# The jobs of an attention and mixer kernel in another written-out order, with other engines for its evacuations

## The chip, the cores and the metric

One core of a Trainium2 chip runs the whole kernel. The metric is device time in microseconds (us) from the start of an execution to its end. The engines are TensorE (PE in the profile, with weight loads as PEld), VectorE (DVE), ScalarE (ACT), GpSimd (POOL) and SyncE (SP). TensorE writes its products into PSUM, in eight banks, from which DVE or ACT (not POOL here) take them away; such a read is called an evacuation below. DMA transfers are issued from the queues of SP, ACT and POOL and carried by 16 DMA engines.

## The reference

Eight batches, eight heads, 576 positions, 64 channels a head. Attention with 128 positive random features is followed by a token and a channel mixer on rows of 512 channels.

```python
def phi(x):                        # x = q or k, scaled by 64 ** -0.25
    h = einsum('bhsd,md->bhsm', x, omega) - sum(x * x, -1) / 2
    return exp(h - max(h, -1)) / sqrt(128)
q_p, k_p = phi(q_s), phi(k_s)
kv, z = einsum('bhsm,bhsd->bhmd', k_p, v), k_p.sum(2)
x = einsum('bhsm,bhmd->bhsd', q_p, kv) / (einsum('bhsm,bhm->bhs', q_p, z) + 1e-6)
x = x.transpose(0, 2, 1, 3).reshape(8, 576, 512)
u = x + (relu(x.transpose(0, 2, 1) @ w_tok1) @ w_tok2).transpose(0, 2, 1)
out = u + relu(u @ w_ch1) @ w_ch2  # 512 -> 1536 -> 512
```

## The kernel before

Every batch is cut into 512 main positions and 64 tail positions. The kernel first describes its work as 1528 *jobs* and then issues them. A job is a function that issues a few instructions on one engine, with the jobs that it depends on, the buffers that it takes and those that it frees. `Planner.add` (L155) appends one; its number is its place in the list.

The order of issue is not found when the program is built. `Planner.run` (L182) walks a list of numbers written into the file, `ORDER` (L22), and calls each job's function in turn. Every engine and every DMA queue runs what it was issued in that order, so the list fixes the order of each engine by itself and of SP's, ACT's and POOL's queues of transfers. Two more tables go with it. `SLOT` is a string of digits: the next digit gives the buffer of its ring (or the PSUM bank) whenever a job takes a new one. `MOVED` gives the engine of jobs that do not run on their usual one; `Planner.engine` (L208) looks it up as a job is described. A negative entry n of `ORDER` is no job: it calls `warm(-1-n)` (L1251), one 128x512 product of a tensor of zeros into bank -1-n, whose result nothing reads.

```python
for n in ORDER:
    if n < 0:
        self.warm(-1 - n)
        continue
    j = self.jobs[n]
    ...
    self.go(j)
```

`turns` (L163) makes elementwise jobs of DVE and POOL that use their shared port take turns, by an explicit dependency wherever the two engines alternate.

The stages of a batch b, with the lines that the profile names:

- *Loads.* For batches 0 and 1 q and k come in as rows (L367, L378) and TensorE transposes them (L518, L535, L552). From batch 2 on POOL's queue casts them to 16 bits in DRAM (L407 for q, L412 and L418 for main and tail of k) and SP's queue brings them back transposed (L428) as qT and kT. v is loaded by POOL (L385, L399).
- *Attention.* Features of k (L599, L707) and of q (L719) are products evacuated by exponentials on ACT (L562, and others). DVE reduces (L740) and inverts (L744) for the scale of v, which is multiplied on DVE or POOL (L343, a helper for all elementwise sums and products). TensorE makes kv (L763, L770) and numerators with denominators (L796, L798); DVE inverts the denominators (L803) and DVE or ACT scale (L814, L812), which gives x.
- *Token mixing.* Products L831 and the tail L824 with relu, then L844 (L898 for a pair's tail) and on DVE the addition of x (L847), which gives u. From batch 2 on SP's queue transposes u (L852) as uT, its only wait being the four additions. Batches 0 and 1 have their own version (L870, L871, L882, L884) in which TensorE gives uT itself.
- *Channel mixing.* Batches 0 and 1: products L1178 and L1212. From batch 2 on the two products are split into 2 by 2 blocks and made as seven products of sums of blocks: L1107 on the way in with sums of uT (POOL or DVE) and of the weights, evacuated by DVE (L1131) and ACT (L338), and L989 on the way out with sums S and T of the hidden blocks (POOL or DVE, L343), added up by DVE in `o` (L969). Stores go out from SP, ACT or POOL (L1024, L1036).

The list overlaps batches: while channel mixing of one batch runs, attention of the next batch or the one after it is laid between its products. In the list before, channel mixing of batch c starts at these job numbers: 178 (batch 0), 463 (batch 2), 641 (batch 3). The jobs that the prediction speaks of by their place are 634 (transpose of u of batch 3, on SP), 717 and 893 (transposes of k of batches 4 and 5, on SP), 890 and 891 (the casts that 893 depends on, on POOL), 154 (first token product of batch 0), 459 and 460 (two sums of uT of batch 2), 0 (the identity on POOL, `make_identity`) and 10 (a load of rows on POOL's queue).

Of the kernel before, what the change touches and what calls it, by code (L numbers as in the profile page):

```python
# [22 lines left out]
    2, 38, 16, 3, 7, 6, 4, 9, 12, 10, 0, -8, 41, 1, 14, 39, 42, 40, 47, 48, 8, 11, 13, 21, 22, 19, 17, 5, 78, 49,  # L23
    129, 43, 79, 80, 50, 131, 130, 44, 18, 45, 46, 95, 54, 96, 97, -1, 51, 69, -3, 112, 52, 55, 113, 114, 84, 135,
    56, 53, 28, 73, 70, 101, 118, 102, 136, 119, 120, 103, 137, 132, -8, 81, -3, 74, 71, 75, 133, 76, -1, -1, -3,
    -1, 57, 115, 82, 72, 116, 134, 59, -8, -8, -2, 104, 117, 121, 138, 98, 83, 105, 30, 25, 23, 24, 77, 20, 33, 31,
    29, 85, 58, 122, 139, 100, 99, 86, -1, 126, 140, 123, 143, 87, 88, 141, 124, 127, 125, 128, 144, 145, 63, 106,
    92, 89, 154, 109, 142, 158, 65, 159, 90, 107, 155, 93, 110, 91, 108, 94, 156, 111, 64, 208, 15, 160, 146, 161,
    147, 157, 253, 66, 209, 150, 67, 151, 255, 211, 210, 254, 68, 148, 152, 149, 153, 60, 270, 219, 178, 186, 271,
    272, 220, 221, 187, 179, 184, 212, 62, 61, 213, 259, 276, 236, 256, 216, 238, 237, 218, 258, 182, 172, 176, 180,  # L30
    217, 173, 257, 177, 214, 225, 260, 185, 277, 183, 242, 226, 243, 278, 261, 222, 239, 273, 32, 241, 240, 275,
    170, 168, 171, 27, 353, 26, 351, 215, 162, 279, 163, 262, 244, 274, 224, 280, 165, 356, 357, 263, 223, 164, 181,
    227, 284, 281, 264, 282, 265, 267, 166, 245, 174, 169, 246, 175, 167, 285, 266, 283, 247, 228, 268, 269, 229,
    286, 188, 230, 250, 233, 251, 248, 231, 252, 249, 232, 234, 235, 189, 193, 198, 287, 194, 290, 288, 289, 457,
    34, 291, 203, 294, 292, 296, 298, 199, 195, 200, 293, 295, 297, 299, 35, 36, 196, 451, 352, 355, 403, 386, 358,
    354, 453, 300, 535, 536, 190, 204, 191, 405, 201, 388, 387, 404, 420, 369, 359, 421, 361, 422, 360, 205, 370,
    389, 366, 391, 301, 303, 368, 367, 371, 304, 390, 323, 319, 320, 307, 308, 206, 315, 392, 409, 426, 362, 427,
    302, 324, 410, 393, 428, 411, 363, 364, 394, 537, 372, 406, 423, 313, 316, 424, 408, 373, 407, 425, 375, 365,
    311, 305, 429, 395, 412, 312, 376, 37, 377, 309, 306, 314, 374, 310, 396, 413, 430, 417, 418, 434, 414, 400,
    397, 431, 378, 435, 436, 401, 419, 415, 432, 321, 379, 383, 380, 416, 384, 398, 381, 385, 399, 382, 325, 317,  # L40
    402, 433, 322, 455, 452, 192, 207, 202, 538, 539, 197, 437, 550, 556, 438, 440, 542, 713, 540, 541, 714, 558,
    326, 439, 441, 551, 557, 552, 327, 454, 318, 456, 329, 331, 458, 333, 335, 336, 715, 328, 332, 334, 330, 444,
    446, 553, 570, 448, 339, 555, 554, 571, 572, 442, 445, 447, 449, 559, 443, 337, 543, 604, 587, 544, 606, 545,
    588, 605, 589, 340, 560, 576, 342, 341, 546, 338, 547, 548, 577, 343, 610, 344, 611, 450, 607, 590, 573, 592,
    609, 574, 575, 716, 717, 347, 578, 549, 561, 579, 345, 612, 459, 460, 562, 348, 593, 580, 608, 591, 563, 581,
    584, 613, 564, 567, 346, 582, 585, 565, 566, 594, 568, 569, 583, 614, 586, 463, 615, 496, 495, 618, 479, 480,
    466, 498, 468, 500, 619, 616, 620, 595, 461, 462, 617, 482, 499, 483, 501, 497, 596, 464, 469, 597, 502, 503,
    467, 484, 485, 601, 470, 598, 465, 471, 504, 602, 599, 472, 600, 486, 510, 487, 481, 488, 505, 475, 473, 506,
    603, 476, 478, 491, 489, 721, 621, 507, 492, 509, 622, 508, 723, 623, 722, 624, 474, 494, 490, 477, 493, 511,
    515, 512, 513, 625, 349, 519, 350, 891, 1068, 1244, 720, 718, 719, 895, 894, 890, 889, 517, 516, 724, 520, 630,  # L50
    631, 632, 628, 765, 768, 626, 633, 629, 627, 725, 726, 523, 767, 770, 766, 769, 524, 782, 748, 728, 784, 749,
    750, 783, 729, 730, 634, 525, 526, 734, 731, 751, 732, 752, 733, 753, 771, 772, 754, 527, 755, 531, 788, 528,
    737, 532, 738, 727, 514, 773, 756, 518, 637, 739, 893, 892, 896, 638, 1069, 774, 757, 635, 775, 735, 758, 736,
    641, 776, 762, 759, 779, 777, 763, 780, 636, 760, 789, 529, 521, 764, 761, 522, 530, 644, 778, 781, 897, 907,
    899, 908, 909, 898, 657, 642, 658, 924, 785, 790, 640, 1067, 639, 645, 660, 926, 740, 646, 787, 741, 786, 925,
    673, 674, 900, 913, 901, 661, 930, 662, 791, 643, 745, 647, 742, 648, 676, 792, 793, 663, 678, 664, 649, 679,
    677, 794, 902, 746, 795, 743, 650, 796, 653, 747, 797, 665, 680, 659, 666, 651, 903, 675, 744, 534, 1071, 533,
    681, 669, 667, 685, 798, 654, 670, 686, 652, 682, 672, 931, 668, 683, 932, 799, 941, 958, 800, 802, 942, 656,
    959, 960, 943, 801, 803, 684, 688, 655, 687, 671, 693, 689, 695, 691, 697, 698, 944, 904, 927, 946, 905, 906,
    929, 945, 808, 806, 701, 810, 804, 933, 699, 934, 928, 964, 807, 809, 811, 805, 961, 1075, 1119, 1077, 1076,  # L60
    962, 1120, 963, 1121, 812, 1070, 1074, 1072, 1249, 1073, 1245, 696, 694, 690, 702, 965, 966, 704, 935, 938, 700,
    914, 915, 947, 936, 939, 937, 948, 705, 703, 916, 940, 917, 967, 968, 692, 949, 910, 1136, 1085, 709, 911, 912,
    1086, 1137, 1087, 918, 972, 950, 951, 833, 1125, 1078, 1079, 706, 1080, 1126, 919, 710, 969, 952, 955, 973, 974,
    970, 956, 957, 953, 954, 707, 921, 817, 818, 920, 971, 1138, 922, 923, 975, 1102, 978, 820, 1104, 1103, 836,
    979, 815, 1127, 813, 814, 1142, 1143, 1144, 1248, 1081, 816, 976, 977, 822, 838, 1082, 1122, 708, 821, 1108,
    1091, 823, 1084, 1124, 1083, 986, 982, 824, 980, 1145, 1128, 983, 981, 1109, 987, 1129, 825, 839, 1123, 819,
    849, 852, 984, 834, 829, 826, 1130, 827, 840, 830, 985, 837, 854, 841, 1131, 1092, 828, 1132, 835, 842, 850,
    1133, 1134, 853, 1110, 1093, 855, 856, 831, 857, 832, 845, 851, 843, 1135, 848, 858, 844, 864, 861, 1094, 846,
    862, 1095, 1146, 859, 860, 847, 863, 1247, 712, 711, 988, 1261, 1139, 1088, 989, 1111, 990, 1112, 1263, 1262,
    1090, 1140, 1089, 1141, 873, 1278, 1251, 1105, 1252, 1279, 1253, 1107, 1106, 996, 1012, 1011, 995, 1027, 869,  # L70
    1250, 874, 871, 865, 867, 993, 991, 1113, 998, 1280, 1030, 1014, 999, 1254, 1114, 1115, 1243, 992, 994, 870,
    866, 1246, 1423, 877, 1028, 1000, 1016, 1116, 1032, 1147, 1015, 1001, 1002, 1117, 1031, 1148, 1118, 878, 1149,
    997, 1017, 1033, 1013, 1018, 1034, 1096, 1003, 1099, 1007, 1019, 1004, 1035, 1008, 880, 1005, 1284, 1100, 1020,
    1255, 1006, 1101, 1150, 1039, 1151, 1021, 879, 1029, 1097, 1256, 881, 1098, 1022, 1152, 1040, 1153, 1295, 1023,
    868, 872, 1036, 882, 1267, 1042, 1268, 1285, 885, 1154, 1037, 1156, 1026, 1009, 1296, 1024, 1025, 1297, 1157,
    1155, 883, 1038, 1301, 1041, 886, 1257, 1269, 1286, 884, 1302, 1010, 1298, 1281, 1312, 1300, 1282, 1283, 1313,
    1314, 1299, 1162, 1163, 1043, 1044, 1303, 1160, 1164, 1158, 1051, 1165, 1161, 1159, 1264, 1315, 1258, 1424, 888,
    1166, 1422, 1259, 1260, 875, 1318, 1287, 1319, 1052, 1045, 1047, 1049, 1053, 1266, 1288, 1316, 1265, 1317, 1292,
    1289, 1270, 1055, 1304, 1048, 1290, 1271, 876, 1305, 1320, 887, 1272, 1275, 1321, 1050, 1167, 1168, 1046, 1169,
    1170, 1309, 1293, 1056, 1273, 1054, 1058, 1276, 1310, 1274, 1311, 1322, 1291, 1323, 1326, 1306, 1324, 1294,  # L80
    1277, 1307, 1327, 1328, 1308, 1325, 1203, 1172, 1171, 1204, 1329, 1187, 1206, 1330, 1331, 1190, 1059, 1174,
# [1204 lines left out]
```

## Time and profile before

| | us |
|---|---|
| three runs | 268.26, 268.55, 269.92 |
| their median | 268.55 |
| the profiled execution, its own time | 270.67 |
| its span, first to last instruction | 268.9 |
| mean granted TensorE clock in it | 0.998 |
| DMA traffic | 39.72 MB in 81826 packets, mean 148 GB/s |

The page gives busy time of each engine as a share of the span. The other views used are: the waits of an engine (what ended each idle stretch: total us, times, longest), busy time in stretches (length, then each engine's busy us with its instructions, the granted clock, the mean busy share of the DMA engines, GB/s), the chain that ended last (start, length, what), and an engine's timeline (start, length, line, operation, out<-in, count, and in brackets the idle time ahead with what ended it). A DMA's line on its queue's timeline is the time the queue took to issue it; the transfer itself goes on behind that. Matmuls overlap, so busy times of neighbours in a timeline do; from start to start is the better measure.

### The profile page before, as it was taken

The numbers are of one execution on the slowest core, as the hardware profiler recorded it, in microseconds if no ns is written. First come the engines' busy times: TensorE is split into PE (matmuls) and PEld (weight loads), VectorE is DVE, ScalarE is ACT, GpSimd is POOL, SyncE is SP. The second block draws the span as 40 slices with busy tenths as digits, with TensorE's granted clock in tenths as the row PEclk, the third lists the DMA queues.
The fourth block names the chain that finished last, engine by engine and source line by source line (L and its number), as shares of the span: only waits on it lengthen the run. The fifth ranks groups of instructions, "written<-read, shape, count | busy, mean of one in ns | idle before, by whom it ended". The sixth has DMA issues, their size and how long they took to land.

```text
span 268.9 us, 6989 instructions
## 1 busy us (share of the span) xinstructions
PE 257.9 (96%) x2752; PEld 190.6 (71%) x2752; DVE 231.7 (86%) x494; ACT 183.0 (68%) x425; POOL 158.9 (59%) x160
## 2 busy tenths in 40 slices
PE   4999999999999999989999999999999999999993
PEld 2568455454667985768768777897696788888882
DVE  3999978599999998889999999998987898788982
ACT  1997982089885896879988989878865482273400
POOL 8765553061897966987498852745775004927171
PEclk9999999999999999999999999999999999999999
DMA  7999999999999999999999927844350513040144
GB/s 192 199 208 200 205 207 184 175 220 186 240 168 143 175 207 187 121 198 210 175 222 189 240 85 80 119 85 95 105 152 0 80 67 112 0 157 4 41 146 127
DMA packets 81826, 39.72 MB, mean 148 GB/s; under 512 B 64033, under 2 KB 77729, under 8 KB 81601
## 3 DMA queue, kind: packets, MB, share of 16 engines
q0 software_dynamic: 31712, 17.61, 44.7%
q1 hardware_dynamic: 48560, 19.50, 34.7%
q10 hardware_dynamic: 1520, 2.16, 2.3%
q8 instruction: 21, 0.34, 0.5%
q14 instruction: 13, 0.10, 0.1%
HBM read 35.95 MB, written 16.52 MB: 195 GB/s over the span
## 4 chain that ended last, share of the span: by engine, by line
PE 81%; DMA 7%; POOL 6%; issue 2%; DVE 2%; ACT 1%; POOLq 0%
PE bank L989 23%; PE bank L1107 21%; PE bank L1178 7%; PE bank L1212 4%; PE bank L831 4%; PE bank L844 4%; DMA k<-in_k_dram 4%; DMA uT<-u 3%; PE bank L707 3%; PE bank L796 3%; PE bank L763 2%; PE bank L719 2%; POOL S L343 2%; POOL vs L343 1%; POOL uT L343 1%
## 5 line engine op out<-in xcount | busy, mean ns | idle before, releaser
L562 ACT ACTIVATE kp<-bank 128x512 f16<-128x512 f32 x64 | 35.8, 610 | 13.5 <-PE bank L707 13.1
L338 ACT ACTIVATE r<-bank 128x512 f16<-128x512 f32 (+1 forms) x50 | 29.1, 606 | 20.1 <-PE bank L1107 9.9
L989 PEld LDWEIGHTS <-r 128*128 128x128 f16 x384 | 36.9, 98 | 6.8 <-issue 1.0
L562 ACT ACTIVATE qp<-bank 128x512 f16<-128x512 f32 x64 | 36.7, 631 | 2.5 <-PE bank L719 2.4
L740 DVE TENSOR_REDUCE km<-kp 128x8 f16<-128x1024 f16 x32 | 38.1, 1205 | 0.5 <-ACT kp L562 0.5
L343 POOL TENSOR_TENSOR vs<-v,vs 128x512 f16<-128x512 f16 x22 | 23.7, 1082 | 16.0 <-DVE vs L744 5.5
L1107 PE MATMUL bank<-uT,wc 128*128 128x256 f16 x228 | 30.5, 273 | 1.2 <-DMA uT<-u 1.2
L989 PEld LDWEIGHTS <-S 128*128 128x128 f16 x288 | 27.6, 98 | 4.4 <-POOL S L343 0.2
L1107 PEld LDWEIGHTS <-wc 128*128 128x128 f16 x252 | 23.5, 98 | 5.7 <-DMA uT<-u 1.7
L343 POOL TENSOR_TENSOR S<-r,S 128x768 f16<-128x768 f16 x15 | 24.4, 1641 | 4.5 <-DVE vbd L644 3.4
L989 PE MATMUL bank<-T,r 128*128 128x256 f16 x192 | 23.8, 273 | 0.1
L989 PE MATMUL bank<-T,S 128*128 128x256 f16 x192 | 23.6, 273 | 0.0
L989 PE MATMUL bank<-wc,r 128*128 128x256 f16 x192 | 23.4, 273 | 0.0
L812 ACT ACTIVATE x<-bank,rc 128x64 f16<-128x64 f32 x100 | 22.4, 348 | 0.4 <-DVE rc L803 0.4
L343 POOL TENSOR_TENSOR uT<-uT,uT 128x512 f16<-128x512 f16 x10 | 11.6, 1158 | 17.9 <-PE bank L1107 15.8
L338 ACT ACTIVATE r<-r 128x512 f16<-128x512 f16 (+1 forms) x21 | 16.7, 822 | 7.5 <-DVE r L1131 7.5
L1107 PE MATMUL bank<-uT,qT 128*128 128x256 f16 x126 | 21.7, 272 | 0.0
L847 DVE TENSOR_TENSOR u<-x,bank 128x512 f16<-128x512 f16 x28 | 17.8, 680 | 4.3 <-PE bank L844 4.2
L1107 PE MATMUL bank<-uT,kT 128*128 128x256 f16 x126 | 21.4, 273 | 0.0
L1178 PE MATMUL bank<-uT,wc 128*128 128x512 f16 x88 | 20.5, 380 | 0.0
L969 DVE TENSOR_TENSOR o<-u,bank 128x512 f32<-128x512 f16 x28 | 19.0, 677 | 1.8 <-PE bank L989 1.7
L814 DVE TENSOR_TENSOR x<-bank,rc 128x320 f16<-128x320 f32 x44 | 20.0, 477 | 0.4
(158 smaller groups left out, 612.5 us busy)
## 6 DMA issues: line engine op xcount, KB each, us to landing
out_dram<-o SPq DMA_DIRECT2D x11, 512.0 KB, 4.5
q<-in_q_dram POOLq DMA_DIRECT2D x6, 576.0 KB, 9.2
wc<-in_moe_w_ch_dram POOLq DMA_DIRECT2D x4, 768.0 KB, 13.1
k<-in_k_dram POOLq DMA_DIRECT2D x6, 512.0 KB, 9.4
v<-in_v_dram POOLq DMA_DIRECT2D x6, 512.0 KB, 8.9
out_dram<-o SPq DMA_DIRECT2D x6, 256.0 KB, 3.3
r<-in_q_dram POOLq DMA_DIRECT2D x4, 288.0 KB, 7.6
v<-in_v_dram POOLq DMA_DIRECT2D x4, 256.0 KB, 10.8
```

The source lines that it names most:

```text
L338: nc.scalar.activation(out=out, in_=in_, func=AF.Relu)
L343: (nc.gpsimd if eng == "POOL" else nc.vector).tensor_tensor(**kw)
L562: nc.scalar.activation(out=out, in_=in_, func=AF.Exp, bias=0.0, scale=1.0)
L740: nc.vector.reduce_max(out=t_km[place("km", (b, hp))], in_=src_, axis=AX.X)
L812: nc.scalar.activation(out=to[:, j], in_=ps[:, j], func=AF.Copy, scale=rc[:, j : j + 1])
L814: nc.vector.tensor_tensor(out=to, in0=ps, in1=rc.unsqueeze(2).broadcast_to((P, NJ + 1, D)), op=ALU.mult)
L831: nc.tensor.matmul(ps, w1m[:, j, tb * P : (tb + 1) * P], x[:, j, :], start=False, stop=(j == NJ - 1))
L847: nc.vector.tensor_tensor(out=t_u[place("u", b)][:, j, :], in0=t_x[place("x", b)][:, j, :], in1=bank(n), op=ALU.add)
L969: nc.vector.tensor_tensor(out=o, in0=a, in1=ps, op=ALU.add)
L989: nc.tensor.matmul(ps[:, j * DH : (j + 1) * DH], a[:, cb, j * P : (j + 1) * P], w[:, cb, :], start=(bank_of(b, j0) not in held and j == j0 ...
L1107: nc.tensor.matmul(ps[:, n, :], w(a)[:, (2 * m + n) * P : (2 * m + n + 1) * P], x_[:, a], start=(what in ("P1", "P2", "P5") and n == 0 and ...
L1178: nc.tensor.matmul(ps, wc1[:, db, cb * P : (cb + 1) * P], moving(db), start=(db == 0), stop=(db == ND - 1))
```

## The change

It rewrites the three tables and nothing else. `ORDER` goes from 1541 to 1535 entries: the same 1528 jobs in another order, with 7 warm-up products instead of 13 (the one ahead of job 41 is among those that go). `SLOT` has 850 digits as before, dealt anew. `MOVED` goes from 155 to 179 entries, with which 140 jobs change their engine. Among these are evacuations of the first transposes and kv (58, 61, 64, 67, 68, 122, 139 to ACT), relus and scalings swapped between DVE and ACT throughout, weight sums (451, 454, 456, 457, 458 to POOL; 452 and 455 to DVE), the sums 459 and 460 of uT (POOL to DVE), scalings of v (227, 244, 377 to DVE; 394, 411, 428 to POOL), and the queues of some stores. Job 0 goes ahead of load 10. On SP's queue 893 goes ahead of 634, on POOL's queue 890 and 891 go ahead of most other loads and casts of their neighbourhood.

```diff
@@ -20,112 +20,114 @@
 ORDER = [
-    2, 38, 16, 3, 7, 6, 4, 9, 12, 10, 0, -8, 41, 1, 14, 39, 42, 40, 47, 48, 8, 11, 13, 21, 22, 19, 17, 5, 78, 49,
...
-    515, 512, 513, 625, 349, 519, 350, 891, 1068, 1244, 720, 718, 719, 895, 894, 890, 889, 517, 516, 724, 520, 630,
...
-    750, 783, 729, 730, 634, 525, 526, 734, 731, 751, 732, 752, 733, 753, 771, 772, 754, 527, 755, 531, 788, 528,
-    737, 532, 738, 727, 514, 773, 756, 518, 637, 739, 893, 892, 896, 638, 1069, 774, 757, 635, 775, 735, 758, 736,
...
+    7, 2, 38, 3, 9, 12, 0, 41, 16, 1, 14, 39, 42, 40, 6, 47, 48, 4, 10, 8, 11, 13, 21, 22, 19, 17, 5, 78, 49, 129,
...
+    890, 891, 894, 588, 589, 613, 345, 562, 593, 348, 346, 552, 551, 614, 579, 615, 618, 459, 616, 617, 619, 460,
...
+    729, 767, 730, 1068, 889, 720, 718, 719, 893, 895, 1244, 517, 516, 523, 726, 524, 731, 782, 751, 526, 783, 752,
...
+    788, 738, 518, 727, 756, 773, 514, 757, 774, 635, 758, 898, 775, 734, 907, 924, 529, 634, 896, 739, 892, 1069,
...
 ]
 SLOT = (
...
 )
 MOVED = {
-    42: "DVE", 44: "ACT", 46: "ACT", 50: "DVE", 52: "ACT", 55: "ACT", 59: "ACT", 65: "ACT", 86: "DVE", 88: "ACT",
...
-    428: "DVE", 430: "DVE", 433: "ACT", 452: "POOL", 453: "POOL", 455: "POOL", 459: "POOL", 460: "POOL", 478: "ACT",
...
+    42: "DVE", 44: "ACT", 46: "ACT", 52: "ACT", 55: "ACT", 58: "ACT", 59: "ACT", 61: "ACT", 64: "ACT", 65: "ACT",
...
+    334: "POOL", 377: "DVE", 379: "DVE", 396: "DVE", 399: "ACT", 402: "ACT", 413: "DVE", 430: "DVE", 433: "ACT",
+    451: "POOL", 453: "POOL", 454: "POOL", 456: "POOL", 457: "POOL", 458: "POOL", 478: "ACT", 514: "POOL",
...
 }
```

More of the change, by code (lines that the diff above doesn't have):

```diff
@@ L113 @@
-    261: "DVE", 269: "ACT", 278: "DVE", 280: "DVE", 291: "DVE", 312: "DVE", 318: "DVE", 324: "DVE", 328: "POOL",
-    330: "POOL", 332: "POOL", 334: "POOL", 349: "ACT", 394: "DVE", 396: "DVE", 402: "ACT", 411: "DVE", 413: "DVE",
-    428: "DVE", 430: "DVE", 433: "ACT", 452: "POOL", 453: "POOL", 455: "POOL", 459: "POOL", 460: "POOL", 478: "ACT",
-    509: "ACT", 510: "ACT", 514: "POOL", 516: "POOL", 517: "POOL", 518: "POOL", 586: "ACT", 595: "DVE", 603: "ACT",
-    617: "ACT", 637: "POOL", 638: "POOL", 639: "POOL", 640: "POOL", 656: "ACT", 690: "POOL", 692: "POOL",
@@ L118 @@
-    694: "POOL", 696: "POOL", 744: "ACT", 778: "ACT", 781: "ACT", 798: "ACT", 813: "POOL", 814: "POOL", 815: "POOL",
-    816: "POOL", 831: "ACT", 832: "ACT", 866: "POOL", 868: "POOL", 869: "POOL", 870: "POOL", 920: "ACT", 940: "ACT",
-    971: "ACT", 992: "POOL", 994: "POOL", 1009: "ACT", 1025: "ACT", 1026: "ACT", 1041: "ACT", 1043: "POOL",
-    1044: "POOL", 1046: "POOL", 1050: "POOL", 1066: "ACT", 1101: "ACT", 1112: "DVE", 1152: "ACT", 1167: "POOL",
-    1168: "POOL", 1169: "POOL", 1170: "POOL", 1174: "DVE", 1185: "ACT", 1186: "ACT", 1202: "ACT", 1217: "ACT",
@@ L123 @@
-    1220: "POOL", 1222: "POOL", 1224: "POOL", 1226: "POOL", 1271: "DVE", 1277: "ACT", 1291: "ACT", 1325: "ACT",
-    1333: "DVE", 1348: "POOL", 1355: "DVE", 1362: "DVE", 1363: "ACT", 1373: "DVE", 1380: "ACT", 1387: "DVE",
-    1395: "ACT", 1396: "ACT", 1397: "POOL", 1398: "POOL", 1400: "POOL", 1404: "POOL", 1426: "POOL", 1427: "POOL",
-    1429: "POOL", 1445: "ACT", 1449: "DVE", 1461: "ACT", 1477: "ACT", 1480: "POOL", 1481: "POOL", 1485: "POOL",
-    1514: "ACT", 1516: "POOL", 1517: "POOL", 1518: "ACT", 1519: "SP", 1520: "ACT", 1521: "SP", 1524: "ACT",
@@ new lines @@
+    308: "DVE", 310: "DVE", 312: "DVE", 314: "DVE", 318: "DVE", 320: "DVE", 328: "POOL", 330: "POOL", 332: "POOL",
+    334: "POOL", 377: "DVE", 379: "DVE", 396: "DVE", 399: "ACT", 402: "ACT", 413: "DVE", 430: "DVE", 433: "ACT",
+    451: "POOL", 453: "POOL", 454: "POOL", 456: "POOL", 457: "POOL", 458: "POOL", 478: "ACT", 514: "POOL",
+    516: "POOL", 517: "POOL", 518: "POOL", 566: "ACT", 595: "DVE", 597: "DVE", 600: "ACT", 603: "ACT", 620: "ACT",
+    637: "POOL", 638: "POOL", 639: "POOL", 640: "POOL", 688: "ACT", 690: "POOL", 692: "POOL", 694: "POOL",
@@ new lines @@
+    696: "POOL", 761: "ACT", 764: "ACT", 778: "ACT", 795: "ACT", 813: "POOL", 814: "POOL", 815: "POOL", 816: "POOL",
+    832: "ACT", 866: "POOL", 868: "POOL", 869: "POOL", 870: "POOL", 872: "POOL", 923: "ACT", 937: "ACT", 951: "DVE",
+    957: "ACT", 971: "ACT", 1008: "DVE", 1009: "ACT", 1010: "ACT", 1042: "ACT", 1043: "POOL", 1046: "POOL",
+    1047: "POOL", 1048: "POOL", 1050: "POOL", 1098: "ACT", 1101: "ACT", 1115: "ACT", 1129: "DVE", 1132: "ACT",
+    1146: "DVE", 1149: "ACT", 1167: "POOL", 1168: "POOL", 1169: "POOL", 1170: "POOL", 1174: "DVE", 1184: "DVE",
@@ new lines @@
+    1185: "ACT", 1186: "ACT", 1201: "ACT", 1206: "DVE", 1209: "DVE", 1216: "DVE", 1217: "ACT", 1220: "POOL",
+    1222: "POOL", 1226: "POOL", 1241: "ACT", 1308: "ACT", 1311: "ACT", 1325: "ACT", 1345: "POOL", 1347: "POOL",
+    1348: "POOL", 1363: "ACT", 1379: "ACT", 1380: "ACT", 1389: "DVE", 1396: "ACT", 1399: "POOL", 1401: "POOL",
+    1404: "POOL", 1420: "ACT", 1427: "POOL", 1428: "POOL", 1449: "DVE", 1460: "ACT", 1465: "DVE", 1470: "DVE",
+    1475: "DVE", 1481: "POOL", 1483: "POOL", 1485: "POOL", 1514: "ACT", 1515: "SP", 1516: "POOL", 1517: "POOL",
@@ L129 @@
+    1518: "ACT", 1519: "SP", 1520: "ACT", 1522: "ACT", 1523: "SP", 1525: "SP", 1526: "ACT", 1527: "SP",
 }
```

25 lines of the change are left out of this document (13 added, 12 removed), and 140 rows, old and new, of the table ORDER.

## The prediction

> **What bounds the kernel now.** I read the page's first part first, then the waits of TensorE, then busy time in stretches of 20 us, then the chain that ended last.
>
> ```profile
> span 268.9 us, 6989 instructions
> PE 257.9 (96%) x2752; PEld 190.6 (71%) x2752; DVE 231.7 (86%) x494; ACT 183.0 (68%) x425; POOL 158.9 (59%) x160
> ```
>
> TensorE is busy for 257.9 of 268.9 us, so only 11.0 us of its time is empty, and the change leaves its 1528 jobs as they are. A reordering can win only from those 11.0 us, and from warm-up matmuls that count as busy.
>
> ```profile
> PE bank L518 <- POOL S masks.py:199: 2.7, 1, 2.7
> PE bank L1107 <- DMA uT<-u: 1.2, 1, 1.2
> PE bank L1252 <- DVE S L1249: 1.2, 1, 1.2
> PE bank L599 <- DMA kT<-k: 0.7, 1, 0.7
> PE bank L707 <- ACT kT L334: 0.5, 1, 0.5
> ```
>
> (Total us, times, longest.) Three of these waits lie in the first 10 us. Two come later and are both DMAs: channel mixing of batch 3 waits 1.2 us for the transposed u (L1107), and the first products with keys of batch 4 wait 0.7 us for their transpose (L599).
>
> ```profile
> 0.00:20.00 20.00, 15.26 (x223) 9.63 (x224) 14.73 (x38) 14.12 (x33) 15.41 (x28) 1.00 1.05 200
> 20.00:40.00 20.00, 20.00 (x245) 12.24 (x242) 17.61 (x41) 17.28 (x41) 10.09 (x13) 1.00 1.25 204
> ...
> 100.00:120.00 20.00, 17.97 (x194) 12.54 (x192) 16.89 (x33) 15.21 (x36) 15.53 (x15) 1.00 1.27 162
> ...
> 240.00:260.00 20.00, 20.00 (x185) 17.91 (x184) 17.79 (x35) 6.37 (x12) 10.46 (x8) 1.00 0.14 50
> 260.00:269.00 9.00, 4.62 (x42) 3.81 (x40) 3.69 (x9) 0.00 (x0) 2.27 (x3) 0.94 0.58 168
> ```
>
> After the stretch's length the first figure is TensorE's busy time. Of the twelve stretches from 20 to 260 us, eleven are full (first and last shown) and one lacks 2.03 us: 100 to 120. The rest of the emptiness is the head (4.74 us) and the tail (4.38 us).
>
> **What the change does to the time.** It edits three tables: the order of issue, the buffer of each write, and the engine of 140 evacuations and sums. I take its parts by place.
>
> *The two stalls at 101 and 117 us.*
>
> ```profile
> 100.28 0.38 PE L1107 MATMUL bank<-uT,sum 128*128 128x256 f16 x2
> 101.37 0.29 PE L599 MATMUL bank<-omT,kT 64*128 64x128 f16 x4 [0.70 <-DMA kT<-k]
> ...
> 107.22 0.62 PE L844 MATMUL bank<-r,w 128*128 128x512 f16 x2
> ...
> 115.58 0.62 PE L898 MATMUL bank<-r,w 128*64 128x512 f16 x4
> 117.41 0.61 PE L1107 MATMUL bank<-uT,wc 128*128 128x256 f16 x4 [1.21 <-DMA uT<-u]
> ```
>
> ```profile
> 90.33 3.34 SPq L428 DMA_TRANSPOSE kT<-k  x1
> ...
> 108.60 4.15 SPq L852 DMA_TRANSPOSE uT<-u  x1
> 112.93 4.37 SPq L428 DMA_TRANSPOSE kT<-k  x1
> ```
>
> ```profile
> 106.09 2.48 DVE L847 TENSOR_TENSOR u<-x,bank 128x512 f16<-128x512 f16 x4
> ```
>
> ```profile
> 108.60 8.76 DMA uT<-u
> ...
> 118.02 0.12 PE bank L796 x4
> ...
> 118.63 2.62 PE bank L989 x24
> ...
> 121.47 0.22 PE bank L707 x8
> ...
> 123.44 0.22 PE bank L719 x2
> ```
>
> The last fence is the chain, the one before it DVE's timeline, and ahead of that SP's, with the time its queue took to issue. SP issues the transpose of u at 108.60, when DVE's last addition ends (106.09 + 2.48 = 108.57). It takes 8.76 us. In before's order TensorE has 8.6 us of its own work between the last L844 products of batch 3 (107.22) and the product that needs the transpose (117.41, or 10.2 later), and it runs out. The new order puts 24 more L989 products between (2.62 us), four L719 (0.44), sixteen L707 (0.44), ten L796 and L798 (0.30), four L599 (about 0.1), and more switches between 64- and 128-row matmuls (0.2): 4.1 us more, 12.7 in all. What is needed is 1.4 us from those products to the issue (107.22 to 108.60) and 8.76: 10.2 us. So this wait should go, with 2.5 us to spare. The transpose of k for batch 4 stands third behind the u of batch 2 in SP's queue. In the new order the last L844 of batch 2 comes about 4 us of TensorE work sooner; I let 2.3 us reach the k transpose (issued at 88.0 for 90.33) since DVE's additions and the cast of q do not all follow. Its first use moves 1 us sooner, so that the 0.7 us go, barely.
>
> A stall costs more than its idle time, for the pipeline drains. L989's 2.62 us for 24 give 0.109 a product, so after two L1107 products at 100.28 the next could start at 100.50; it started at 101.37, 0.87 lost. Four L898 at 115.58 give way at 116.02; the next started at 117.41, 1.39 lost. Together 2.3 us. Bounds: 0 if both stay, 2.3 if both go. **I take −2.3.**
>
> *The head.*
>
> ```profile
> L1252 PE MATMUL bank<-S 128*128 128x512 f16 x12 | 3.9, 382 | 0.2 <-ACT kpt L611 0.2
> ```
>
> ```profile
> 31.14 3.56 PE bank L1178 x16
> ```
>
> ```profile
> 2.74 1.14 POOL r L367 x2
> ...
> 12.61 2.25 DVE km L740 x2
> ```
>
> ```profile
> 20.14 0.39 PE L870 MATMUL bank<-x,w1m 128*128 128x128 f16 x4
> ```
>
> Six of the 13 warm-up matmuls are dropped, the one ahead of all transposes among them (the row is cut to 8 to 28 us and has the other 12). A matmul of 512 columns takes 0.22 us of the queue (3.56 by 16), so 1.3 us of filler goes. POOL makes its identity masks one load earlier, half of 1.14 us, so that the first transposes may start 0.57 us sooner. But neither is at the end of the chain. That runs from the exponentials through DVE's reduction (12.61) to the scaled v, the numerators, their division and the token mixing, whose first product starts at 20.14. Following the new order by hand with the durations of before, instruction by instruction on DVE, ACT and TensorE, I get 19.95, from where TensorE has the same 7.5 us of work up to the first channel product. Bounds: −1.9, if identity and warm-up count in full (0.57 + 1.3), and +0.6, if ACT's or DVE's new order in the head adds one evacuation to that chain. **I take −0.2**, since the chain holds DVE and ACT, whose work is unchanged.
>
> *140 jobs on other engines.* Added up job by job by their durations in the trace of before, DVE goes from 229.0 to 229.9 us, ACT from 177.1 to 176.8, POOL from 157.5 to 158.9: each about 1 us or less. They lie under TensorE's 257.9 as long as banks come free in time. DVE is tightest between the additions of batches 2 and 3: 26.6 us of its work to 27.7 of TensorE's, where before had 24.2 to 25.6. If the cover is gone there, each evacuation costs its length.
>
> ```profile
> L847 DVE TENSOR_TENSOR u<-x,bank 128x512 f16<-128x512 f16 x28 | 17.8, 680 | 4.3 <-PE bank L844 4.2
> ```
>
> That is 0.68 us for one such read. Row switches of TensorE go from 82 to 79, nothing. Bounds: 0 to +2 (three evacuations late). With the next part **I take +0.3** for both.
>
> *SP's and POOL's queues.* The transpose of k for batch 5 now stands ahead of the transpose of u for batch 3, and its casts stand earlier in POOL's queue.
>
> ```profile
> 90.14 1.16 POOL L343 TENSOR_TENSOR uT<-uT 128x512 f16<-128x512 f16 x1
> 91.37 1.16 POOL L343 TENSOR_TENSOR uT<-uT,uT 128x512 f16<-128x512 f16 x1
> 92.47 0.59 POOL L412 DMA_DIRECT2D k<-in_k_dram  x1
> ```
>
> ```profile
> 93.05 9.76 DMA k<-in_k_dram
> ```
>
> The two sums at 90.14 and 91.37 move to DVE, so the casts are issued by about 90.1. After 9.76 us they have landed, at 99.9, and SP can issue the transpose. The first use comes 8.4 us of TensorE work sooner than the 121.2 of before, less the 2.3 us of stalls that no longer precede it: about 110.3.
>
> ```profile
> uT<-u SPq DMA_TRANSPOSE x7, 5.6
> kT<-k SPq DMA_TRANSPOSE x6, 6.8
> ```
>
> With the median of 6.8 us it lands at 106.7, with the 11.0 of the k transpose that was issued at 90.33 (needed at 101.37, 0.70 of it idle) at 110.9. So the cost is 0 to 0.6.
>
> **Sum:** −2.3 − 0.2 + 0.3 = −2.2. The profiled execution took 270.67 us, 1.77 more than its span of 268.9; its span becomes 266.7 and its time 268.5. The median of the runs, 268.55, lies 2.1 below it, so I forecast 268.55 − 2.2 = **266.4**.
>
> The page "DMA: Bandwidth & Descriptors" of the Trainium skill says, under "Queues, rings and completion order", that each DMA engine takes packets from its queues in turn. By that a service time belongs to the mix that ran beside it, and an order searched with times from a trace need not find them again. The rows agree so far: transposes of k have a median of 6.8 and one took 11.0, with POOL's casts beside it.
>
> **The rivals.** *A, the head shortens in full.* For it: TensorE is busy for 15.26 of the first 20 us with the fillers counted in, and the identity is what its first transposes wait for (2.7 us, L518). Against it: the chain through DVE at 12.61. It gives −1.9 instead of −0.2: **264.7**.
>
> *B, the waits move.* The transposes that are now pulled forward, k of batch 5 above all, share the DMA engines with the same casts, whose load is highest in the stretch from 100 to 120 (1.27, the column ahead of the last). If k of batch 5 lands 1.9 us after its first use (112.2 instead of 110.3; issued at 99.9 it would then have taken 12.3 us, where the slowest of its kind took 11.0, or have been issued later), one stall stands for two: 266.4 + 1.9 = **268.3**, no change.
>
> *C, slower: the queue order on SP.* If POOL reaches the casts late, k's transpose holds SP, and u of batch 3 waits behind it. From casts issued at x, the transpose starts at x + 9.76, holds SP for 4.37, and u lands 8.76 later, x + 22.9. TensorE needs it at about 116.9, so it decides from x = 94.0, and each us later costs one. At x = 97.6 it is 3.6 us: **270.0**. For it: POOL's sums ahead of the casts wait on DVE's port turns. Against it: POOL drops 2.3 us of sums there, and x should be 90.
>
> *D, the change does not do what it says.* The stalls at 101 and 117 stay since their DMAs now take longer by as much as they start earlier: 266.4 + 2.3 − 0.2 = **268.5**.
>
> *E, the clock of TensorE.* Fewer warm-up matmuls could leave it low for longer.
>
> ```profile
> 6.54 0.61 PE L707 MATMUL bank<-omT,kT 64*128 64x128 f16 x8
> ...
> 9.76 0.40 PE L707 MATMUL bank<-omT,kT 64*128 64x128 f16 x8 [0.45 <-ACT kT L334]
> ```
>
> The same eight products took 0.61 and later 0.40 us, so the clock opens between. If it opened 4 us later, work of some 4 us would cost half as much again, +2: **268.4**. The page "TensorE: Matmul & The Clock Gate" of the Trainium skill, in its account of the gate, ties it to sustained activity, and by that dropping fillers speaks against this change. The row of the fillers shows 12 of the 13 behind 8 us (its view is cut to 8 to 28), so that one alone lies ahead of the opening; the drop of that one is what the trace leaves open.
>
> **How the numbers follow.** Forecast 0.52 (own range 265.3 to 267.5), A 0.13, B 0.17, C 0.08, D 0.06, E 0.04. Faster by over 1% means under 265.9, about what a measurement of this kernel can tell: a third of the forecast's 0.52 and all of A give 0.30. Slower by over 1% is over 271.2: half of C and the far ends of B and E, 0.08. Within: 0.62. The range of 8 in 10 leaves out half of A below (264.5) and most of C above: 264.5 to 269.6.
>
> **What would show it.** Right: TensorE full from 20 to 260 us, no wait for uT<-u or kT<-k above 0.5 us, its first L870 at 19.5 to 20.2 and its first L1178 near 27.5, the tail after the last product unchanged. A would show L870 below 19; B a wait on kT<-k near 110; C a transpose of u issued after 108 with TensorE waiting on it; D the old two waits; E L707 groups of 0.6 us after 9 us. I am wrong if a wait of over 1 us stands anywhere after 20 us, or if TensorE's busy time grows.

## The result and the profile after

The changed kernel takes 272.58 us (median of four executions: 272.29, 272.43, 272.72 and 285.33), the kernel before 268.4 in the same comparison: a ratio of 1.0139, 95% interval 1.01 to 1.0178, so it is 1 to 2% slower. The prediction said 266.4 us, between 264.5 and 269.6. Some executions of the changed order (285.33 is one), and of most experiments below, ran into a longer stall of the kind described in the last section, which adds 10 to 30 us; the ratios given leave such executions out.

The page after, its first two parts, and the waits of TensorE (line numbers are two higher than before's):

```profile
span 270.5 us, 7003 instructions
PE 258.0 (95%) x2746; PEld 191.1 (71%) x2746; DVE 233.7 (86%) x499; ACT 183.6 (68%) x448; POOL 160.0 (59%) x160
```

```profile
PE bank L520 <- POOL S masks.py:199: 4.1, 1, 4.1
PE bank L601 <- DMA kT<-k: 2.7, 1, 2.7
PE bank L991 <- DVE o L971: 0.5, 1, 0.5
PE bank L798 <- DVE kvsb L336: 0.3, 1, 0.3
PE bank L991 <- POOL S L345: 0.2, 1, 0.2
```

Busy time in stretches of 20 us:

```profile
20.00:40.00 20.00, 19.67 (x224) 11.62 (x222) 17.10 (x34) 18.63 (x41) 11.20 (x13) 1.00 1.25 203
40.00:60.00 20.00, 19.98 (x171) 10.16 (x172) 16.19 (x37) 8.03 (x25) 8.66 (x9) 1.00 1.20 197
...
100.00:120.00 20.00, 16.71 (x181) 11.21 (x178) 16.16 (x31) 14.05 (x34) 12.76 (x11) 1.00 1.39 190
120.00:140.00 20.00, 20.00 (x229) 16.01 (x226) 19.11 (x46) 19.37 (x52) 15.08 (x17) 1.00 1.09 179
```

TensorE's busy time is the same to 0.1 us (257.9 and 258.0). The wait for the transposed u is gone as forecast, the one near 101 us too. In their place stands one wait of 2.7 us for the k transpose of batch 5, and the stretch from 100 to 120 us, the only one with more than 0.4 us missing between 20 and 260, lacks 3.29 us. The other 0.6 us of it are two waits on sums:

```profile
108.13 1.16 PE L991 MATMUL bank<-T,S 128*128 128x256 f16 x9 [0.18 <-POOL S L345]
110.51 1.47 PE L991 MATMUL bank<-T,r 128*128 128x256 f16 x12 [0.46 <-DVE o L971]
```

SP's timeline and the chain there:

```profile
90.39 3.71 SPq L430 DMA_TRANSPOSE kT<-k  x1
94.20 1.31 SPq L1038 DMA_DIRECT2D out_dram<-o  x2
101.80 7.21 SPq L430 DMA_TRANSPOSE kT<-k  x1
109.06 7.11 SPq L854 DMA_TRANSPOSE uT<-u  x1
```

```profile
101.80 14.63 DMA kT<-k
```

The transpose was issued at 101.80 and landed 14.63 us later, at 116.43; its first product had been free to start at about 113.8 (it starts at 116.48 after 2.65 us of waiting).

### The profile page after: what moved, and what is told of

The parts are those of the page before. It is cut to its first block, busy times and chain, and to the rows that moved or that the text cites. A ratio compares the mean times of both kernels' runs of the same rounds, so it can differ in the third digit from the quotient of the medians.

```text
span 270.5 us, 7003 instructions
## 1 busy us (share of the span) xinstructions
PE 258.0 (95%) x2746; PEld 191.1 (71%) x2746; DVE 233.7 (86%) x499; ACT 183.6 (68%) x448; POOL 160.0 (59%) x160
## 4 chain that ended last, share of the span: by engine, by line
PE 84%; DMA 5%; DVE 4%; ACT 2%; issue 1%; POOL 1%; DVEq 0%; POOLq 0%
PE bank L991 26%; PE bank L1109 24%; DMA kT<-k 5%; PE bank L1180 4%; PE bank L833 4%; PE bank L1214 4%; PE bank L846 4%; PE bank L798 3%; PE bank L765 3%; PE bank L709 3%; PE bank L721 2%; DVE km L742 2%; PE bank L520 1%; DVE vs L345 1%; PE bank L900 1%
## 5 line engine op out<-in xcount | busy, mean ns | idle before, releaser
L814 ACT ACTIVATE x<-bank,rc 128x64 f16<-128x64 f32 x135 | 30.5, 346 | 3.7 <-DVE rc L805 3.4
L345 POOL TENSOR_TENSOR vs<-v,vs 128x512 f16<-128x512 f16 x22 | 22.8, 1054 | 15.6 <-DVE r L342 4.0
L340 ACT ACTIVATE r<-bank 128x512 f16<-128x512 f32 (+1 forms) x42 | 24.8, 615 | 10.7 <-PE bank L833 5.4
L1109 PE MATMUL bank<-uT,wc 128*128 128x256 f16 x228 | 31.4, 273 | 0.0
L345 POOL TENSOR_TENSOR r<-r 128x768 f16<-128x768 f16 x10 | 16.3, 1637 | 14.6 <-DVE S L345 11.4
L340 ACT ACTIVATE r<-r 128x512 f16<-128x512 f16 (+1 forms) x15 | 12.5, 834 | 9.8 <-DVE r L1133 8.9
L816 DVE TENSOR_TENSOR x<-bank,rc 128x320 f16<-128x320 f32 x37 | 16.9, 477 | 0.3
```

The costliest lines, as they stand in the source:

```text
L340: nc.scalar.activation(out=out, in_=in_, func=AF.Relu)
L345: (nc.gpsimd if eng == "POOL" else nc.vector).tensor_tensor(**kw)
L814: nc.scalar.activation(out=to[:, j], in_=ps[:, j], func=AF.Copy, scale=rc[:, j : j + 1])
L816: nc.vector.tensor_tensor(out=to, in0=ps, in1=rc.unsqueeze(2).broadcast_to((P, NJ + 1, D)), op=ALU.mult)
L1109: nc.tensor.matmul(ps[:, n, :], w(a)[:, (2 * m + n) * P : (2 * m + n + 1) * P], x_[:, a], start=(what in ("P1", "P2", "P5") and n == 0 and ...
```

## The experiments

Jobs by number, all of this neighbourhood: 890 and 891 cast k of batch 5, 893 transposes it; 1068 and 1244 cast the tails of k of batches 6 and 7, 889 q of batch 5; 720, 718 and 719 load v of batch 4, 894 and 895 tails of v of batch 5; 517 and 516 are sums on POOL that run from about 106 us. "Burst" is what POOL's queue issues between 89 and 106 us.

### The kernel before in another execution

e1 is the kernel before, unchanged (no edit).

> The kernel before, unchanged, profiled once more. Theory 1 (the two waits of 0.7 and 1.2 us on the transposes near 101 and 117 us were those of the one slow execution that was profiled, 270.67 us against a median of 268.5): span near 266.6 us, no wait of TensorE on a transposed k or u above 0.3 us after 20 us. Theory 2 (they are there in every execution, and the change lost its time elsewhere): the two waits again, span near 268.9 us or shorter by something else.

It took 268.17 us. Its waits, its stretch from 100 to 120 us, and SP's timeline:

```profile
PE bank L518 <- POOL S masks.py:199: 2.7, 1, 2.7
PE bank L1252 <- DVE S L1249: 1.2, 1, 1.2
PE bank L707 <- ACT kT L334: 0.7, 1, 0.7
PE bank L1252 <- ACT kpt L611: 0.2, 1, 0.2
```

```profile
100.00:120.00 20.00, 19.98 (x222) 14.43 (x220) 19.21 (x39) 16.39 (x41) 17.77 (x17) 1.00 1.28 184
```

```profile
89.78 2.57 SPq L428 DMA_TRANSPOSE kT<-k  x1
...
107.87 3.87 SPq L852 DMA_TRANSPOSE uT<-u  x1
111.92 2.84 SPq L428 DMA_TRANSPOSE kT<-k  x1
```

The transpose of 111.92, that of batch 5:

```profile
DMA to landing us min/median/max: 5.8/5.8/5.8
```

Theory 1 holds. The span is 266.4 us, not 268.9, and neither DMA wait is there: the k transpose issued at 89.78 landed in 4.7 us, where it took 11.0 in the execution that the prediction read. The 19 executions of before in that comparison lie between 268.13 and 271.07, median 268.93. Of the two executions with a trace one has both stalls and one has neither; what the others between them have is not shown, and e1's is one of the fastest. Against e1 the change costs 4.1 us of span, and 3.27 of them (19.98 less 16.71) are missing in that one stretch.

### Where in the order the loss is made

e4 takes the changed order, engines and buffers for the first 150 entries, e5 for 510 (82 us); e6 is the reverse, before's for 520 entries.

In short (the lists themselves are written out in full, as in the change):

```
e4: after[:150]  + (before without those)
e5: after[:510]  + (before without those)
e6: before[:520] + (after without those)
```

> The changed order, engines and buffers up to the first 150 entries (the head, to about 22 us), then those of before. Prediction's step on the head (-0.2 us): 268.2 us. If the head pays in full: 266.5 us. If the dropped warm-up products or the moved evacuations cost: 269 us or more, and the first product of channel mixing after 27.9 us.

> The changed order, engines and buffers for its first 510 entries (to about 82 us, ahead of the casts of k for batch 5), those of before from there on. Theory 1 (the loss is made between 100 and 120 us by the later part's transfers and its earlier uses of them): 268.5 us, no wait of TensorE above 1.5 us after 20 us. Rival (the earlier part costs it, by half a us for every 20 us): 270 us or more.

> The reverse: before's order to about 84 us (520 entries), the changed one from there on. Theory 1: 272 us, with a wait of 2 us or more on the k transpose of batch 5 near 114 us. Rival: below 270 us.

e4: 268.77 us, ratio 0.9983 (0.9946 to 1.002), and 268.09 with a span of 266.3 in its profiled execution, against 266.4 of e1. The first product of token mixing starts at 19.67 us there and at 19.70 in the changed kernel (forecast 19.95, before 20.14); the first of channel mixing at 27.60 and 27.28 (before 27.72). The head gives about 0.1 us, too little for these executions to show, and 0.33 of what the changed kernel had gained by 27 us is missing again before 40 (the 19.67 above). e5: ratio 1.0053 (1.0014 to 1.0093); its seven executions without the long stall have a median of 270.86, where theory 1 had 268.5 and the rival 270. Its profile has two waits of 1.0 us that neither kernel has, for scaled v near 89 us and for an output block near 115, so the run doesn't clear the part up to 82 us; the changed kernel's own stretches do, with 0.35 us missing between 20 and 100. e6: ratio 1.0142 (1.0044 to 1.0239), the same as the change itself, with the k transpose of batch 5 at 15.9 us; but the wait for it was 0.6 us, where theory 1 asked for 2 or more, and its largest wait was 1.9 us for scaled v at 90 us, just behind its joint, which neither kernel has. So the two halves don't place the loss: both add waits of their own. What places it is the changed kernel's trace, where 3.27 of the 4.1 us against e1 are missing between 100 and 120.

### Taking the wait away at TensorE

e3 leaves all transfers where they are and uses the transpose later.

```diff
-785, 768, 897, 754, ..., 899, ..., 898, 775, 734, 907
+785, 768, 754, ..., 775, 734, 897, 899, 898, 907
```

> The changed kernel with the first product that needs the k transpose of batch 5 (and its two exponentials) put 2.6 us of TensorE work later, behind twelve products, two kv groups, the pair's tail and one group of features; no transfer is moved. Theory 1: the wait of 2.7 us goes, nothing else changes, 269.7 us. Rival: the wait turns up at the next user or as a wait for the transposed u of batch 3, whose issue SP's queue holds behind it: 271 to 272.4 us.

Seven of ten executions took 271.0 to 273.3 us, median 271.62 (272.01 with the three that ran into the long stall), ratio 1.01 (1.0067 to 1.0133): the rival's time, though the wait that turned up is neither of the two it named. The transpose itself took 14.9 us, as before the edit. PE's and POOL's timelines of e3:

```profile
115.68 0.40 PE L768 MATMUL bank<-vs,kp 128*128 128x65 f16 x8 [1.25 <-POOL vs L348]
116.69 0.40 PE L768 MATMUL bank<-vs,kp 128*128 128x65 f16 x8 [0.55 <-POOL vs L348]
```

```profile
113.56 1.06 POOL L348 TENSOR_TENSOR vbd<-vt,vbd 128x512 f16<-128x512 f16 x1 [2.96 <-DMA vt<-in_v_dram]
114.57 2.07 POOL L348 TENSOR_TENSOR vs<-v,vs 128x512 f16<-128x512 f16 x2
```

The wait for k is gone and TensorE waits 1.8 us for scaled v of batch 4 instead, because POOL waits for the loads of v. The main load, first in the changed kernel (issued at 94.60), then in e1 (96.24):

```profile
DMA to landing us min/median/max: 18.3/18.3/18.3
```

```profile
DMA to landing us min/median/max: 8.4/8.4/8.4
```

The cast of q took 13.6 us for 8.4, and POOL, whose queue was held up, reached its first sum of the neighbourhood at 106.42 instead of 104.50; the two short waits on sums above follow from there. So the transpose was not late alone: the transfers beside it were late too.

### Is it what runs beside the transpose?

e9 is the kernel before with two moves in queues and none on TensorE.

```diff
 POOL's queue
-891, 1068, 1244, 720, 718, 719, 895, 894, 890, 889, 517
+891, 890, 1068, 1244, 720, 718, 719, 895, 894, 889, 517
 SP's queue
-634, 893, 892
+893, 634, 892
```

> The kernel before with two moves in queues alone: the tail casts of k for batch 5 go right behind its main cast on POOL's queue, and its transpose goes ahead of the transpose of u for batch 3 on SP's queue. TensorE's order is untouched, so the k transpose is not needed before 121 us. Theory 3 (a transpose that is issued into a flood of POOL's casts and loads that have not landed slows with all of them): it is issued near 101 us instead of 112 and takes 12 us or more instead of 6 to 7, the loads beside it take longer too, and the transposed u of batch 3 or v of batch 4 comes late: 270 to 273 us. Rival (service times belong to the transfers, and 14.6 us was due to the late cast): it takes 6 to 8 us, and the time stays at 268.5 to 269 us.

281.0 to 293.7 us, median 290.94, all four with the long stall. SP's timeline, the k transposes issued between 99 and 113 us, the chain, the stretches, and TensorE's wait:

```profile
101.45 7.22 SPq L431 DMA_TRANSPOSE kT<-k  x1
108.72 23.68 SPq L855 DMA_TRANSPOSE uT<-u  x1
```

```profile
DMA to landing us min/median/max: 31.1/31.1/31.1
```

```profile
103.41 29.18 DMA out_dram<-o
```

```profile
104.00:108.00 4.00, 4.00 (x35) 2.54 (x33) 3.90 (x9) 1.79 (x5) 3.24 (x2) 1.00 1.55 128
108.00:112.00 4.00, 4.00 (x52) 3.04 (x51) 3.38 (x5) 3.59 (x7) 0.00 (x0) 1.00 1.77 64
112.00:116.00 4.00, 0.54 (x12) 0.29 (x9) 0.00 (x0) 2.17 (x5) 0.49 (x1) 0.88 1.47 46
116.00:120.00 4.00, 0.00 (x0) 0.00 (x0) 0.00 (x0) 0.00 (x0) 3.16 (x3) 0.50 1.47 58
120.00:124.00 4.00, 0.00 (x0) 0.00 (x0) 0.00 (x0) 0.00 (x0) 0.00 (x0) 0.50 1.96 58
124.00:128.00 4.00, 0.00 (x0) 0.00 (x0) 0.00 (x0) 0.00 (x0) 0.00 (x0) 0.50 0.77 73
```

```profile
PE bank L992 <- DVE o L972: 20.9, 1, 20.9
```

The same transpose that takes 5.8 us at 111.92 in e1 takes 31.1 at 101.45, and a store of ACT's queue issued beside it, at 103.41, takes 29.18. The DMA engines stay busy (0.77 to 1.96) and move 46 to 73 GB/s from 108 to 128 us. No product that TensorE had reached needed that transpose; TensorE stood because DVE's next sum `o` waited for the store to free its buffer. Theory 3 holds against a service time that belongs to the transfer: the transpose, issued into the burst, slows with everything beside it, and far more than the transfers would take one after the other by e1's times. In e1 SP issues the transpose of k at 111.92, when the burst has landed (its last transfer, the cast of q, took 8.4 us from 103.41); that of u, at 107.87, still ran beside this one cast and took 6.7 us.

The k transpose of batch 4, issued near 90 us, shows the same without an experiment of its own. In e1, e4, e5 and e9 it was issued 2.2 to 2.9 us ahead of POOL's first cast there and took 4.7 to 4.9 us; in e6 and e11, 0.2 to 0.4 us ahead, it took 7.1 and 7.7; in the changed kernel, e3, e7, e8, e10, e14 and e15 it was issued within a us behind that cast and took 9.1 to 12.8. The lead alone doesn't settle the time: with 2.3 us in e13 it took 6.7, and with 2.1 in the execution that the prediction read 11.0.

e11 is e6 with the three casts that nobody needs yet moved behind the sums; e13 is e9 with the cast of q alone moved so.

```diff
 e11, POOL's queue
-890, 891, 894, 1068, 889, 720, 718, 719, 895, 1244, 517, 516
+890, 891, 894, 720, 718, 719, 895, 517, 516, 1068, 889, 1244
 e13, POOL's queue
-891, 890, 1068, 1244, 720, 718, 719, 895, 894, 889, 517, 516
+891, 890, 1068, 1244, 720, 718, 719, 895, 894, 517, 516, 889
```

> Before's order to about 84 us, the changed one behind, and in it the three casts that nobody needs yet (tails of k for batches 6 and 7, q of batch 5) behind two sums on POOL. Without the three the k transpose of batch 5 had 16.0 us. Theory 3: with only the loads of v beside it, it takes 6 to 9 us and its wait (0.6 us) goes; q of batch 5 may come late instead. Rival: 12 us or more.

> The kernel before with the k transpose of batch 5 issued early (as in the run where it took 31 us), and the cast of q for batch 5 (576 KB, the largest of the transfers beside it) put behind two sums on POOL, so that it starts near 107 us instead of 103. If that cast is what the transpose cannot share the engines with: the transpose takes 6 to 9 us, and 269 to 272 us in all. Rival (any of POOL's transfers does it, or their number): 12 us or more, and a wait of TensorE of 3 us or more between 105 and 135 us.

The k transposes issued between 99 and 113 us, first of e6, then of e11:

```profile
DMA to landing us min/median/max: 15.9/15.9/15.9
```

```profile
DMA to landing us min/median/max: 8.6/8.6/8.6
```

Three casts fewer beside it bring the transpose from 15.9 to 8.6 us. The time doesn't follow (275.56 to 296.6 us): the casts then run beside the next transpose, that of q, which took 25.4 us and cost 9.8 us of wait, and 8.5 more came for a k transpose. In e13 the transpose still took 23.5 us (277.2 to 282.4 us): the cast of q is not the only partner.

### Other moves of the burst

e2 puts the same three casts late in the changed kernel; e7 puts v of batch 4 ahead of two of them; e8 is e7 with e3's later use.

```diff
 e2, POOL's queue
-890, 891, 894, 1068, 889, 720, 718, 719, 895, 1244, 517, 516
+890, 891, 894, 720, 718, 719, 895, 517, 516, 1068, 889, 1244
 e7 and e8
+890, 891, 894, 720, 718, 719, 1068, 889, 895, 1244, 517, 516
```

> The changed kernel with three casts on POOL's queue that nobody needs yet (keys of batch 6 and 7, tails, and q of batch 5) issued behind two sums instead of ahead of the transpose of k for batch 5. Theory 1a (this transpose took 14.6 us because other transfers ran beside it): it takes 8 to 10 us, TensorE's wait of 2.7 us for it goes, 269.7 us (272.4 less 2.7). Theory 1b (it is late because its own cast landed at 101.6, and slow whatever runs beside it): wait of 2 us or more stays, 272 us. Theory 2 (the loss is not here): within 0.5 us of 272.4.

> The changed kernel with the load of v for batch 4 (main and tails) put ahead of the casts of k's tail for batch 6 and of q for batch 5 on POOL's queue; the casts of k for batch 5 stay ahead of all. The load should land at 107 to 109 us instead of 113 to 114. Theory 1 alone (the transpose of k for batch 5 sets the loss): its wait of 2.7 us stays, 272 us. Theory 1c (what counts is that the queue brings what is needed first): the transpose has fewer bytes beside it and takes 10 to 12 us, 270.5 us.

> Both: v of batch 4 ahead in POOL's queue, and the first use of the k transpose of batch 5 put 2.6 us of work later. The later use alone left TensorE waiting 1.8 us for the scaled v, whose load came late. Theory 1c: neither wait is left, 269 us (271.6 less 2.2 to 2.8). Rival (another transfer turns up late in place of it): 270.5 us or more, with a third wait between 110 and 125 us.

Medians of 302.0, 286.33 and 290.7 us, every execution with the long stall, so that none of the three theories can be read from the times. In e7 the transpose took 27 us and TensorE waited 6.4 us for it and 7.3 us for sums on POOL. In e2 the stall came before the edit: the k transpose of batch 3, issued at 71.85 beside the previous burst (from 71.61), took 18.3 us, where e1's was issued at 68.93 and took 6.7.

### One cast

e14 moves the cast of q for batch 5 alone; e15 is the same kernel again, for its profile.

```diff
 POOL's queue of the changed kernel
-890, 891, 894, 1068, 889, 720, 718, 719, 895, 1244, 517, 516
+890, 891, 894, 1068, 720, 718, 719, 895, 1244, 517, 516, 889
```

> The changed kernel with the cast of q for batch 5 alone put behind the same two sums. If that cast is the partner: the k transpose of batch 5 takes 6 to 9 us instead of 14.6, v of batch 4 lands by 109 us, and the time is 269.5 us (272.4 less 2.8). Rival: 12 us or more, and 271.5 us or more.

> The changed kernel with the cast of q for batch 5 alone put late, once more for its profile: half of its executions took 268.5 to 269.2 us, but the one that was profiled was not among them. In such an execution: if the k transpose of batch 5 was relieved by the move, it takes 6 to 10 us and TensorE's stretch from 100 to 120 us is full; if it stays at 12 us or more, v of batch 4 landing sooner is not enough to explain the time, and a wait of 1 us or more on the k transpose stays.

Five of e14's ten executions have the long stall (282 to 293 us; the profiled one waited 10.1 us for a later k transpose). The other five took 268.52 to 269.2 us, ratio 0.9973 (0.9932 to 1.0013). e15 took 269.15 us, span 267.4. Its waits, its stretch from 100 to 120 us, and its k transpose of batch 5:

```profile
PE bank L523 <- POOL S masks.py:199: 4.0, 1, 4.0
PE bank L801 <- DVE kvsb L339: 0.3, 1, 0.3
PE bank L604 <- DMA kT<-k: 0.3, 1, 0.3
PE bank L712 <- ACT kT L339: 0.2, 1, 0.2
```

```profile
100.00:120.00 20.00, 19.72 (x217) 14.14 (x215) 19.12 (x38) 16.97 (x42) 15.51 (x15) 1.00 1.32 183
```

```profile
DMA to landing us min/median/max: 11.9/11.9/11.9
```

The transpose took 11.9 us instead of 14.6, and v of batch 4 14.1 instead of 18.3. Of the 3.27 us, 3.01 are back (16.71 to 19.72). It was neither of the two outcomes that were set: the transpose is far from 6 to 10 us, but it was issued 0.6 us sooner (at 101.21), took 2.7 us less, and its first use lacks 0.3 us instead of 2.7. So in an execution without the long stall, the place of this one cast in POOL's queue accounts for the loss; the move does not make the long stall rarer (five of ten, one of four in the changed kernel).

### Two that did not work

e10 undoes the pull of batch 5 in the changed kernel; e12 swaps two transposes in the kernel before.

```diff
 e10, POOL's and SP's queue, and TensorE
+891, 1068, 1244, 720, 718, 719, 895, 894, 890, 889, 517
+634, 893, 892
+641, 673, 657, 897, 642, ..., 658, 907, 924
 e12, SP's queue
-450, 716, 717
+450, 717, 716
```

> The changed kernel with the pulled-forward part of batch 5 put back: its casts and loads in before's order on POOL's queue, the k transpose behind that of u of batch 3, and the three products that use it behind the first products of channel mixing of batch 3. Everything else stays changed. Theory 1 (this is the whole loss): 268.5 us, transposes of 6 to 9 us between 100 and 120 us, no wait above 1 us there. Rival (the earlier and later parts cost as well): 270 us or more.

> The kernel before with one swap on SP's queue: the transpose of k for batch 4 goes ahead of that of q for batch 4 (k is used near 101 us, q near 107). Theory 3: the k transpose then runs ahead of POOL's flood that starts at 92.4 us and lands by 93, so that TensorE's wait for it near 101 us, which some executions of before have, is gone; the q transpose takes its place in the flood with 6 us to spare. Median 268.3 to 268.6 us, and fewer times above 270. Rival (the wait was no matter of overlap, or q or u of batch 3 comes late now): 269 us or more.

e10: three of four executions took 276.5 to 277.5 us, ratio 1.0276 (1.0228 to 1.0325). The k transpose, issued at 114.05 behind that of u and behind the burst, took 4.8 us (that of u, from 109.96, 6.1), but TensorE waited 5.4 us in six places, for ACT and DVE above all, most of it between 122 and 129 us. The pull can't be undone by itself, so the run settles only the transpose's own time. e12: ratio 1.0009 (0.9977 to 1.004), median 269.45, with times up to 271.1 as before, so the rival's outcome: the swap keeps the k transpose out of the burst (5.4 us in its profile) and changes nothing that can be measured. What lets some executions of before take 271 us is not settled. No version was found that beats the kernel before.

## Why the prediction was wrong

- **The two stalls (−2.3 us), the step that failed first.** For the transpose of u the mechanism was right: with the products laid between, it landed 4.0 us ahead of its first use in the changed kernel (at 118.96 for 122.97) and still 1.2 us ahead in e15, where no wait of 2.7 us puts the use off (118.5 for 119.69), though it took 9.7 to 9.9 us. For the transpose of k of batch 4 it was luck: it was issued at 90.39, not at 88.0, took 10.6 us, and no wait appeared only because its first use came at 101.7 instead of 100.7, later and not 1 us sooner. And most of the gain does not exist for a usual execution: e1, without either stall, takes 268.17 us, so that of the median execution (268.93) at most 0.8 us can be such stalls. The prediction itself noted that the profiled execution stood 2.1 us above the median, explained nothing by it, and then took 2.3 us off the median. Against e1, the two stalls are nearly all of what that execution had more.
- **The k transpose of batch 5 (0 to 0.6 us), the term that was mis-sized.** The casts were issued about when forecast (89.6 to 91.8 for 90.1). The transpose was issued at 101.80 for 99.9 and took 14.63 us, where the upper bound used the slowest row, 11.0, so that it landed 5.5 us behind that bound (116.4 for 110.9). The first use came 3.5 us later than forecast too (113.8 for 110.3: it moved 5.1 us against e1's 118.9, not 8.4), and this second error hid part of the first; the wait was 2.7 us. The slowest row was taken for the worst that a transpose of k can do; e9's 31.1 shows that it is no such bound. It is a time for a place between other transfers, and the change moved the transpose into the burst.
- **The new waits (+0.3 us)** were 3.3 us: this one (2.7) and 0.6 us for sums behind POOL's late queue; once the first was removed in e3, the load of v took its place. The change put the cast of q, 576 KB, ahead of that load in POOL's queue. The prediction listed the queue moves and costed none but the one of the casts of k.
- **The head (−0.2 us)** agrees as far as it can be told: 0.1 us in e4's profile, with its first token product 0.3 us sooner than the forecast had it. Warm-up and identity went into idle time: the wait for POOL's mask is 4.1 us for 2.7 and 1.2 of before.
- **140 jobs on other engines (nothing, part of the +0.3)** was right as far as stretches can tell: outside 100 to 120 us TensorE lacks 0.35 us between 20 and 260, though DVE's busy time grew by 2.0 us (231.7 to 233.7) where the sum had 0.9.
- **The rivals.** B was the one: one stall for two, on this transpose. It was priced with a landing at 112.2 us; the transpose landed at 116.43, and the two stalls were not there to be replaced. C's condition (casts behind 94 us) did not occur: SP was held for 7.21 us by the k transpose, to 109.01, but DVE's additions to u ended at 108.78, so this cost 0.2 us. D had the stalls stay; A's full head and E's late clock did not show (sixteen L709 products take 0.69 us at 9.77 and 0.62 at 109).

By the Trainium skill, page "DMA: Bandwidth & Descriptors", section "Queues, rings and completion order", each engine takes packets from its queues in turn. The runs agree that a transfer's time depends on its neighbours (5.8, 14.6 and 31.1 us for one transpose). That sentence doesn't say why all of them together should fall to 58 GB/s, and no run here shows it.

## What to carry to other kernels

Before a stall of a profile is put into a sum, ask whether the execution that was profiled is a usual one: where it lies above the median, the stall may be the difference, and one more profile tells. A transfer's time read from a trace belongs to the transfers beside it, so an order that is searched with such times must not move transfers relative to each other without pricing the overlap anew. Put what is needed first ahead in a queue that runs in order, and, as far as these runs go, keep transposes out of bursts of casts and loads.

## What the runs showed of the hardware that was not expected

With a transpose issued into the burst every queue can be held up: 46 to 73 GB/s for 20 us in e9 (108 to 128), the transfers of POOL's queue issued between 101.5 and 103.5 us take 4.6 to 8.4 us in e1 and 26 to 29 in e9, and in e2 it happened to the burst before. It is a matter of chance and of place: none of the 54 executions of before in four comparisons (of e1, e5, e9 and e12) went above 271.5 us, five of e14's ten did. Which property of the transfers starts it stays open: the cast of q makes it worse (14.6 and 11.9 us) but is not needed (23.5 us in e13).

TensorE's clock follows such a stall. Stretches of e2, whose wait began at 79.3 us:

```profile
80.00:82.00 2.00, 0.00 (x0) 0.00 (x0) 0.64 (x2) 0.00 (x0) 2.00 (x2) 1.00 0.95 77
82.00:84.00 2.00, 0.00 (x0) 0.00 (x0) 0.00 (x0) 0.00 (x0) 1.90 (x2) 0.53 2.19 119
...
94.00:96.00 2.00, 2.00 (x20) 1.47 (x19) 1.81 (x2) 1.63 (x4) 0.00 (x0) 0.55 1.44 155
96.00:98.00 2.00, 2.00 (x19) 1.16 (x17) 1.66 (x5) 1.06 (x3) 0.11 (x1) 1.00 2.08 156
```

The granted clock falls to half about 3 us after TensorE stopped and is back just before 96 us, some 5.5 us after it resumed at 90.25. By an estimate from these rows, 5.5 us at half the clock, this stall of 11 us costs up to 3 more. The page "TensorE: Matmul & The Clock Gate" of the Trainium skill says, in Part 1, that the clock halves after about 3.4 us idle; in the traces it was 2.9 us (e2), 2.5 (e9, stopped at 112.54) and 3.4 (e13, stopped at 112.91), so this or a little less.
